# A one-pass guess matmul, and router logits, marking sum and a transpose set at other places of a hand-written order

## The chip, the cores and the metric

One NeuronCore of one Trainium2 chip. The metric is the device time of one execution in microseconds (us); lower is better. Three timed runs of the kernel before gave 402.77, 403.32 and 403.69 us, median 403.32 us.

## What is computed

Eight batches of a two-step attention, followed by a mixture of eight experts, of which each token uses one. Cut to what matters:

```python
p_packed = sm_attn(p, k, v)               # 32 packed queries per head: [8, 8, 32, 64]
out = sm_attn(q, p_packed, p_packed)      # 576 queries per head attend to the 32 packed rows
x = out as [8 * 576, 512]
logits = x @ w_gate                       # router: [4608, 8]
e_idx = argmax(logits, 1)
gate_w = softmax(logits)[e_idx]
eom = sigmoid(x @ w_output_gate)
out[t] = gate_w[t] * eom[t, e] * (relu(x[t] @ w1[e]) @ w2[e])   # e = e_idx[t]
```

## The kernel before, in words

The kernel bets that nearly all tokens of a batch choose the same expert. For each batch it **guesses** that expert early, runs the dense part for all 576 tokens with that expert's weights, and marks the tokens that chose another; marked tokens are computed again at the end.

For a batch b there are these pieces, each a Python generator that does one step at a time:

- `encode` (letters y, x): scores of the packed queries (`ps_s`), their softmax, its transposition (`ps_a1T`, `ps_a1r`), the **packed values' product** `ps_pp` (L272), its scaled copy `ppc` (VectorE, L277), the **transpose** `ps_ppT` (L285) and its copy `ppT` (ScalarE, L293), the packed rows' gate products `ps_pg` with their copies `pg` (L317, L321), and the guess: a matmul of `pg` with a matrix of ones (`ps_e`, L300) that sums over all packed rows, and six small VectorE steps (L305 to L311) that end in the expert's number.
- `route` (r, t): scores and softmax of the 576 queries (result `a2T`), its split into a high and a low part (`ah`, `al`), the **router logits** `ps_lg` (L398) and their transposition `L` (VectorE, L401), and then `gate`: a first part (L409 to L419, which ends in the exponential `g_ex` on ScalarE), a second part (L423 to L443, with the exponential `g_den` on ScalarE between `g_z` and the reciprocal), the **marking sum** `ps_cnt` (L446, a matmul of the one-hot choices with ones) and the marks (L450 to L457).
- `weights` (w): loads of the guessed expert's w1 and w2; w2 comes in four tiles, each split into `w2h` (ScalarE, L495) and `w2l` (L498, VectorE or GpSimd).
- `values_up` (g): `G`, the packed values times w1 (L513), split into `Gh` (ScalarE) and `Gl` (VectorE), both at the helper's lines L76 and L77.
- `ffn(b)`: the dense part. Two halves of the tokens (256 and 320); in each, eight groups of six matmuls `ps_h` (L85), evicted by ScalarE (`hT`, L579) and VectorE (L582), then the products `ps_o` with w2 (L613; L634 for the last 64 tokens), scaled and evicted by ScalarE (`ob`, L599) and stored.

One **beat** is one batch's `ffn`. Between its steps the letters of a table set what else is issued: `PLANS[b]` says, for step i of beat b, which pieces get one step more. Here y, Y, x work on encode of batches b+1, b, b+2; r and t on route of b+1 and b; w, W on weights of b+1 and b; g on values_up of b+1. Every engine executes its instructions strictly in the order in which this table issues them. The table is all the scheduling there is (`manual_schedule`).

PSUM has eight banks in two groups of four. Group "a" holds attention scores and transposes; group "f" holds `ps_h`, `ps_o`, `ps_lg`, `ps_cnt`, `ps_pg`, `ps_e` and half of `ps_G`. A matmul that opens a bank waits until the bank's last reader has finished. The arrangement of work at the end of beat b, in the second half's steps 28 to 34: product of tokens 256 to 383 (`ps_o` of 24 matmuls), then `ps_pp` of batch b+2 and `ps_G` of batch b+1, then the product of tokens 384 to 511 (again 24 matmuls, called **the last product** below), and then the first `ps_h` group of beat b+1.

Of the kernel before, what the change touches and what calls it, by code (L numbers as in the profile page):

```python
# [11 lines left out]
F32R = mybir.dt.float32r  # L12
# [7 lines left out]
P = 128  # L20
# [6 lines left out]


START = "kkvvqqkkYYYY1YY2YYY3YY4YYtYWttttttyYYt6G7GttGtWtvvqqkkvv"
BESIDE = "8:ry 9:yrr 10:yrrrt 11:yr 12:wrr 13:wrqq 14:rkk 15:r "  # L30
REST = "16:xr 17:x 18:r 19:xvv 20:x 22:x 24:x 25:xxw 26:ww 27:w 28:r 30:r 31:rxg 32:xg 33:gw 34:ww"
PLANS = ["1:GG 3:GG 5:G 6:WW 8:WWW 9:tt 10:tWW 11:Wyy 12:yy 13:tt 14:tt 15:yytt 16:tyy 17:ty 19:y 20:y 21:ryyr 22:yyr "
# [3 lines left out]
         "1:y 2:y 4:yWW 5:y 7:yy 8:ry 9:rry 10:rrry 11:ryw 12:rrw 13:rqq 14:rkkt 15:r " + REST] \  # L36
        + ["0:yW 1:y " + BESIDE + REST] * 3 \
        + ["0:yW 1:y " + BESIDE + REST.replace("16:xr", "20:r"), "0:W 8:l 18:l 20:lt 22:l 23:l 24:l 25:l 27:l 28:l 30:l"]


@with_exitstack
def tile_packed_attn_then_moe(ctx, tc, qT, kT, v, pT, w_go, w1, w2, out):


    nc = tc.nc
    B, _, _, NPAIR, HS = qT.shape
    NG, S = v.shape[1], 2 * HS
    NP = pT.shape[3]
    E, DM, DF = w1.shape[0], out.shape[1], BANK * w1.shape[1] // 2
# [12 lines left out]
    sb = ctx.enter_context(tc.tile_pool(name="sb", bufs=1))  # L62
# [5 lines left out]
    def bank(name, tag="a"):  # L68
        return pool.tile([P, BANK], F32, tag=tag, name=name, bufs=NA if tag == "a" else 8 - NA)

    def f(x):
        return x.bitcast(F32)
# [53 lines left out]
    ones = const.tile([P, P], F32R, name="ones")  # L126
# [44 lines left out]
    R, W, A, G, packed = {}, {}, {}, {}, {}  # L171
# [49 lines left out]
    def encode(b):  # L221
# [62 lines left out]
        ps = bank("ps_ppT")[:, :P]  # L284
# [11 lines left out]
        def guess(of):  # L296

            n = of.shape[1]
            ps = bank("ps_e", "f" if b else "a")[:, :n * E].rearrange("p (g e) -> p g e", e=E)
            nc.tensor.matmul(ps, f(ones), of, start=True, stop=True)  # L300
            yield
            top = sb.tile([P, 2, E], F32, tag="e_top", name="e_top", bufs=1)
            e = ps[:, 0]
            if n > 1:
                nc.vector.tensor_copy(top[:, 1], ps[:, 1])  # L305
                nc.vector.tensor_tensor(top[:, 1], ps[:, 0], top[:, 1], ALU.add)
                e = top[:, 1]
            nc.vector.max(top[:, 0], e)
            nc.vector.max_index(estar_i[:, b], top[:, 0], e)
            if b:  # L310
                nc.vector.tensor_copy(estar_all[:, b:b + 1], estar_i[:, b, 0:1])  # L311
            yield

        if b == 0:
            yield from guess(sums[:, 0:1])
# [3 lines left out]
        R[b] = pg = pgs[b % 3]  # L319
        for g in range(NG):  # L320
            (nc.vector.tensor_copy if b else nc.scalar.copy)(pg[:, g, :2 * E], ps_g[g])  # L321
        yield
        if b:
            yield from guess(pg[:, :, 0:E])

    def route(b):

# [496 lines left out]
    def place(plan, b):  # L824

        kinds = dict(x=(encode, 2), y=(encode, 1), Y=(encode, 0), r=(route, 1), t=(route, 0), u=(route, -1), w=(weights, 1), W=(weights, 0),
                     g=(values_up, 1), G=(values_up, 0), l=(first_leftover, 0))
        for c in plan:
            if c in kinds:
                piece(kinds[c][0], b + kinds[c][1])  # L830
            elif c == "d":
                store()
            elif c.isdigit():
                keep_warm(int(c))
            else:
                fetch(c)
# [68 lines left out]
```

## Time and profile before

| | |
|---|---|
| median of three runs | 403.32 us |
| the profiled execution, whole | 403.31 us |
| its span, first to last instruction | 401.6 us |
| TensorE (PE) busy | 393.9 us, 98% of the span |
| VectorE (DVE) busy | 280.5 us, 70% |
| ScalarE (ACT) busy | 180.7 us, 45% |
| GpSimd (POOL) busy | 40.5 us, 10% |
| share of PE in the chain that ended last | 95% |

The table is the profile's first part and the head of its fourth. Busy time of PE counts from the start of a matmul to its modelled end, so neighbours overlap; a matmul's real cost in a row of matmuls is the distance from its start to the next one's start.

### The profile page before, as it was taken

Reading aid. Unit: us, or ns where it says so; the run is one execution under the profiler, and the core shown is the slowest. Engines: PE = TensorE matmul, PEld = TensorE weight load, DVE = VectorE, ACT = ScalarE, POOL = GpSimd, SP = SyncE. Lnnn points to the kernel's source line nnn. Section 1 sums busy time; section 2 is a strip of 40 time slices with the busy share of each in tenths; the row PEclk is TensorE's granted clock in tenths of the full one; section 3 lists DMA queues with packets and bytes.
Section 4 is the critical chain, followed back from the end, with each engine's and each line's share of the span. In section 5 each row is a group of like instructions: output and inputs, shape, how many; then the busy total and the mean of one; then the engine's idle time right before and its main releaser. Section 6 shows DMA issues by size and latency. Waiting matters only on the chain.

```text
span 401.6 us, 9409 instructions
## 1 busy us (share of the span) xinstructions
PE 393.9 (98%) x3626; PEld 312.7 (78%) x3626; DVE 280.5 (70%) x793; ACT 180.7 (45%) x401; POOL 40.5 (10%) x37
## 2 busy tenths in 40 slices
PE   8999999999999999999999999999999999999995
PEld 2558886879679887787979888788977888798874
DVE  2679789687974977478765886749774786758640
ACT  1455637734555254533726236532645335532300
POOL 7000002420054000200002000020002000010010
PEclk9999999999999999999999999999999999999999
DMA  7899449927970399205990089503951068101921
GB/s 239 333 365 418 153 137 381 398 96 239 412 272 34 106 354 411 89 28 173 395 388 29 10 310 410 231 28 116 357 194 48 14 202 335 42 27 48 374 77 55
DMA packets 36686, 83.60 MB, mean 208 GB/s; under 512 B 3614, under 2 KB 16288, under 8 KB 36640
## 3 DMA queue, kind: packets, MB, share of 16 engines
q1 hardware_dynamic: 36464, 82.85, 55.8%
q8 instruction: 29, 0.48, 0.5%
q10 hardware_dynamic: 144, 0.13, 0.1%
q14 instruction: 17, 0.14, 0.1%
q0 software_dynamic: 32, 0.00, 0.0%
HBM read 67.76 MB, written 15.27 MB: 207 GB/s over the span
## 4 chain that ended last, share of the span: by engine, by line
PE 95%; DVE 2%; DMA 1%; ACT 1%; SPq 0%; issue 0%; DVEq 0%
PE ps_o L613 45%; PE ps_h L85 26%; PE ps_o L634 7%; PE ps_G L92 4%; PE ps_pp L92 3%; PE ps_s2T L92 2%; PE ps_s L92 2%; PE ps_a1T L251 2%; PE ps_lg L92 1%; DMA k<-in_kT_dram 1%; PE ps_lh L739 1%; PE ps_lo L739 1%; PE warm L119 0%; PE ps_e L300 0%; PE ps_h L563 0%; DVE hT L582 0%
## 5 line engine op out<-in xcount | busy, mean ns | idle before, releaser
L613 PE MATMUL ps_o<-w2h,hT 128*128 128x512 f32 x512 | 166.5, 396 | 0.0
L613 PEld LDWEIGHTS ps_o<-w2h,hT 128*128 128x128 f32 x512 | 96.1, 188 | 26.4 <-ACT Gh L76 4.2
L582 DVE SCALAR_TENSOR_TENSOR hT<-ps_h,hT 128x256 fp32r<-128x256 f32 x192 | 60.6, 350 | 58.0 <-ACT hT L579 57.4
L613 PE MATMUL ps_o<-w2l,hT 128*128 128x512 f32 x256 | 100.2, 391 | 0.0
L85 PE MATMUL ps_h<-ah,Gh 128*128 128x320 f32 (+1 forms) x252 | 77.3, 307 | 0.4 <-DVE hT L582 0.2
L85 PE MATMUL ps_h<-ah,Gl 128*128 128x320 f32 (+1 forms) x252 | 74.7, 296 | 0.0
L85 PE MATMUL ps_h<-al,Gh 128*128 128x320 f32 (+1 forms) x252 | 74.6, 296 | 0.0
L579 ACT ACTIVATE hT<-ps_h 128x320 fp32r<-128x320 f32 (+1 forms) x128 | 51.3, 414 | 44.0 <-PE ps_h L85 43.3
L498 POOL TENSOR_TENSOR w2l<-wst,w2h 128x1024 fp32r<-128x1024 f32 x13 | 31.3, 2411 | 299.1 <-ACT w2h L495 270.5
L613 PEld LDWEIGHTS ps_o<-w2l,hT 128*128 128x128 f32 x256 | 48.1, 188 | 9.7 <-DVE w2l L498 0.4
L85 PEld LDWEIGHTS ps_h<-ah,Gh 128*128 128x128 f32 x252 | 47.7, 189 | 4.8 <-issue 1.9
L85 PEld LDWEIGHTS ps_h<-al,Gh 128*128 128x128 f32 x252 | 47.8, 190 | 0.2
L85 PEld LDWEIGHTS ps_h<-ah,Gl 128*128 128x128 f32 x252 | 47.7, 189 | 0.0
L495 ACT CAST w2h<-wst 128x1024 fp32r<-128x1024 f32 (+1 forms) x33 | 33.6, 1047 | 4.3 <-PE ps_o L613 3.0
L599 ACT ACTIVATE ob<-ps_o,scm_all 128x512 f32<-128x512 f32 x27 | 18.5, 686 | 36.1 <-PE ps_o L613 32.9
L498 DVE TENSOR_TENSOR w2l<-wst,w2h 128x1024 fp32r<-128x1024 f32 (+1 forms) x20 | 23.3, 1167 | 7.3 <-ACT w2h L495 7.2
L366 ACT ACTIVATE s<-s 128x576 f32<-128x576 f32 (+2 forms) x18 | 11.4, 633 | 33.1 <-DVE s L363 33.1
L634 PE MATMUL ps_o<-w2h,hT 128*128 128x512 f32 x64 | 25.6, 400 | 0.0
L634 PE MATMUL ps_o<-w2l,hT 128*64 128x512 f32 x64 | 23.9, 394 | 0.0
L77 DVE TENSOR_TENSOR Gl<-ps_G,Gh 128x512 fp32r<-128x512 f32 x28 | 17.4, 681 | 8.0 <-ACT Gh L76 8.0
L386 ACT CAST ah<-a2T 128x576 fp32r<-128x576 f32 (+2 forms) x17 | 10.7, 640 | 24.8 <-DVE a2T L378 24.8
L243 ACT ACTIVATE a<-ps_s,nmx 128x288 f32<-128x288 f32 x32 | 15.8, 506 | 12.6 <-DVE nmx L238 12.5
(190 smaller groups left out, 429.2 us busy)
## 6 DMA issues: line engine op xcount, KB each, us to landing
w<-in_w_dram SPq DMA_DIRECT2D x36, 512.0 KB, 5.5
wst<-in_w_dram SPq DMA_DIRECT2D x36, 512.0 KB, 8.8
vt<-in_v_dram SPq DMA_DIRECT2D x16, 640.0 KB, 8.9
k<-in_kT_dram SPq DMA_DIRECT2D x14, 576.0 KB, 9.8
q<-in_qT_dram SPq DMA_DIRECT2D x14, 576.0 KB, 10.1
out_dram<-ob SPq DMA_DIRECT2D x31, 256.0 KB, 3.6
a_d<-a2T SPq DMA_DIRECT2D x16, 320.0 KB, 8.2
k<-in_kT_dram SPq DMA_DIRECT2D x4, 288.0 KB, 4.8
```

The source lines that it names most:

```text
L77: (lo_eng or nc.vector).tensor_tensor(lo, src, f(hi), ALU.subtract)
L85: res = nc.tensor.matmul(dst, a, m, start=j == 0, stop=j == len(seq) - 1)
L92: res = nc.tensor.matmul(dst, a, m, start=j == 0, stop=j == len(seqs[0]) - 1)
L243: nc.scalar.activation(a1[:, g, hf], s1[hf][g], AF.Exp, bias=nmx[g], scale=QK, accum_out=sm[:, g, hf:hf + 1])
L366: nc.scalar.activation(sf[g], sf[g], AF.Exp, scale=QK)
L495: nc.scalar.copy(h, x)
L498: eng("w", b, j).tensor_tensor(l, x, f(h), ALU.subtract)
L579: nc.scalar.activation(hT[:, :n], ps, AF.Relu)
L582: nc.vector.scalar_tensor_tensor(hT[:, d0:d0 + s1 - s0], ps[:, s0:s1], 0.0, f(hT[:, s0:s1]), op0=ALU.max, op1=ALU.subtract)
L599: nc.scalar.activation(ob, ob if b < 2 and t_ < 2 else ps, AF.Copy, scale=sc)
L613: nc.tensor.matmul(ps, a, m, start=fc == i == 0, stop=fc == FC - 1 and i == 2)
L634: nc.tensor.matmul(ps[:n], a, m, start=i == 0, stop=i == len(seq) - 1)
```

## The change

It moves four things and turns one matmul into another form.

1. For batches 1 to 7 the guess reads a copy `rows` of `pg` in the type float32r, and the ones in the same type. The copy is one more VectorE instruction.
2. In beats 2 to 6 the router logits of batch b+1 move from step 16 (beat 6: step 20) to step 31, behind the packed values' product; their transposition `L` and the gate's two parts move with them, to steps 32, 33 and 34.
3. The marking sum of batch b moves from the end of beat b-1 to step 10 of beat b, behind the guess; the marks to step 12.
4. The transpose `ps_ppT` and the copy `ppT` move from steps 0 and 1 of the next beat to steps 31 and 32, the transpose behind `ps_G`.

```diff
-BESIDE = "8:ry 9:yrr 10:yrrrt 11:yr 12:wrr 13:wrqq 14:rkk 15:r "
-REST = "16:xr 17:x 18:r 19:xvv 20:x 22:x 24:x 25:xxw 26:ww 27:w 28:r 30:r 31:rxg 32:xg 33:gw 34:ww"
+BESIDE = "8:ry 9:yrr 10:yrrr 11:yr 12:wrr 13:wrqq 14:rkk 15:r "
+REST = "16:x 17:x 19:xvv 20:x 22:x 24:x 25:xxw 26:ww 27:w 31:xxrgx 32:xrg 33:gwr 34:wrw"
...
-        + ["0:yW 1:y " + BESIDE + REST] * 3 \
-        + ["0:yW 1:y " + BESIDE + REST.replace("16:xr", "20:r"), "0:W 8:l 18:l 20:lt 22:l 23:l 24:l 25:l 27:l 28:l 30:l"]
+        + ["0:W " + BESIDE.replace("10:y", "10:yt").replace("12:", "12:t") + REST] * 4 \
+        + ["0:W 8:l 10:t 12:t 18:l 20:l 22:l 23:l 24:l 25:l 27:l 28:l 30:l"]
...
-            nc.tensor.matmul(ps, f(ones), of, start=True, stop=True)
+            nc.tensor.matmul(ps, ones if b else f(ones), of, start=True, stop=True)
...
-        yield
         if b:
-            yield from guess(pg[:, :, 0:E])
+            rows = sb.tile([P, NG, E], F32R, tag="e_top", name="rows", bufs=1)
+            nc.vector.tensor_copy(rows, pg[:, :, 0:E])
+        yield
+        if b:
+            yield from guess(rows)
```

Three lines are added ahead of `route`, so from there on a line number of the changed kernel is 3 higher.

TensorE around the last product, end of beat 4, before (rows of `ps_pp` that repeat are left out; `ps_cnt` is the marking sum, `ps_pp` the packed values' product, `ps_o` the last product):

```order
L446 MATMUL ps_cnt<-g_ohq,ones 128x160
L92 MATMUL ps_pp<-vt,a1T 32x64 x16
L92 MATMUL ps_pp<-vt,a1r 32x64 x4
L92 MATMUL ps_G<-w_3250,ppT 32x512 x8
L92 MATMUL ps_G<-w_3253,ppT 32x512 x8
L613 MATMUL ps_o<-w2h,hT 128x512
```

The same place in the changed kernel:

```order
L92 MATMUL ps_pp<-vt,a1T 32x64 x16
L92 MATMUL ps_pp<-vt,a1r 32x64 x4
L92 MATMUL ps_lg<-a2T,pg_94 32x160 x8
L92 MATMUL ps_G<-w_3260,ppT 32x512 x8
L92 MATMUL ps_G<-w_3263,ppT 32x512 x8
L285 MATMUL ps_ppT<-ident,ppc 128x128
L616 MATMUL ps_o<-w2h,hT 128x512
```

The marking sum is gone from here, the logits stand behind the packed values' product, and the transpose, which stood behind the last product, stands in front of it.

ScalarE over the same stretch, before (`low` and the first `ob` belong to the products ahead of `ps_pp`, the second `ob` is the eviction of the last product, `hT` the next beat's groups):

```order
L638 COPY low<-ps_o 64x512
L419 ACTIVATE g_ex<-g_d 128x40
L434 ACTIVATE g_den<-g_z 128x5
L599 ACTIVATE ob<-ps_o,scm_all 128x512
L76 CAST Gh<-ps_G 128x512 x4
L495 CAST w2h<-wst 128x1024 x2
L599 ACTIVATE ob<-ps_o,scm_all 128x512
L579 ACTIVATE hT<-ps_h 128x256
L293 COPY ppT<-ps_ppT 128x128
```

And in the changed kernel:

```order
L641 COPY low<-ps_o 64x512
L602 ACTIVATE ob<-ps_o,scm_all 128x512
L293 COPY ppT<-ps_ppT 128x128
L76 CAST Gh<-ps_G 128x512 x4
L498 CAST w2h<-wst 128x1024
L422 ACTIVATE g_ex<-g_d 128x40
L437 ACTIVATE g_den<-g_z 128x5
L498 CAST w2h<-wst 128x1024
L602 ACTIVATE ob<-ps_o,scm_all 128x512
L582 ACTIVATE hT<-ps_h 128x256 x8
```

The copy `ppT` now stands ahead of the four `Gh`, and the gate's two exponentials stand between the two `w2h`, ahead of the eviction of the last product.

VectorE over the same stretch in the changed kernel, of the gate's small steps only the first and last of each part; before, all the rows named `g_` stood ahead of `ppc`, and the `w2l` directly behind `Gl`:

```order
L277 TENSOR_TENSOR ppc<-ps_pp,rs 128x128
L404 STREAM_TRANSPOSE L<-ps_lg 128x160
L77 TENSOR_TENSOR Gl<-ps_G,Gh 128x512 x4
L412 TENSOR_REDUCE g_mx<-L 128x5
L420 TENSOR_TENSOR g_d<-L,g_mx 128x40
L501 TENSOR_TENSOR w2l<-wst,w2h 128x1024
L426 TENSOR_SCALAR g_cand<-g_d 128x40
L435 TENSOR_REDUCE g_z<-g_og 128x5
L585 SCALAR_TENSOR_TENSOR hT<-ps_h,hT 128x256 x8
```

`g_ex` reads `g_d`, and `g_den` reads `g_z`; a `w2l` of VectorE now stands between them.

## Rows read from the trace of the kernel before

**Rows 1.** The page: busy time of the engines, and TensorE's granted clock in 40 slices.

```profile
PE 393.9 (98%) x3626; PEld 312.7 (78%) x3626; DVE 280.5 (70%) x793; ACT 180.7 (45%) x401; POOL 40.5 (10%) x37
...
PEclk9999999999999999999999999999999999999999
```

**Rows 2.** Busy time by window, one beat: start:end, length, engines, granted clock, DMA.

```profile
216.50:263.00 46.50, 46.50 (x431) 38.04 (x431) 33.08 (x92) 21.86 (x48) 2.35 (x2) 1.00 0.56 213
```

**Rows 3.** Timeline of PE around a guess: start us, length us, instruction, count.

```profile
225.97 0.29 PE L300 MATMUL ps_e<-pg,ones 128*128 128x16 f32 x2
...
226.43 0.39 PE L613 MATMUL ps_o<-w2l,hT 128*128 128x512 f32 x1
```

**Rows 4.** Timeline of PE around marking sums, in beat 2 and in beat 4.

```profile
117.59 0.23 PE L446 MATMUL ps_cnt<-g_ohq,ones 128*128 128x160 f32 x1
...
117.92 0.39 PE L613 MATMUL ps_o<-w2l,hT 128*128 128x512 f32 x1
...
253.64 0.23 PE L446 MATMUL ps_cnt<-g_ohq,ones 128*128 128x160 f32 x1
253.80 0.65 PE L92 MATMUL ps_pp<-vt,a1T 128*32 128x64 f32 x32
```

**Rows 5.** Timeline of PE around router logits, in beats 0, 4 and 6.

```profile
43.39 0.84 PE L92 MATMUL ps_lg<-a2T,pg 128*32 128x160 f32 x16
44.05 0.63 PE L92 MATMUL ps_pp<-vt,a1T 128*32 128x64 f32 x32
...
235.61 0.75 PE L92 MATMUL ps_lg<-a2T,pg 128*32 128x160 f32 x16
236.29 0.42 PE L85 MATMUL ps_h<-ah,Gh 128*128 128x320 f32 x1
...
329.09 0.31 PE L85 MATMUL ps_h<-ah,Gl 128*128 128x320 f32 x1
...
330.26 0.31 PE L85 MATMUL ps_h<-al,Gh 128*128 128x320 f32 x1
```

**Rows 6.** Timeline of PE, last product of beat 4 to the end of beat 5's first groups.

```profile
256.93 0.50 PE L613 MATMUL ps_o<-w2h,hT 128*128 128x512 f32 x1
...
262.53 0.27 PE L285 MATMUL ps_ppT<-ident,ppc 128*128 128x128 f32 x1
262.55 0.36 PE L85 MATMUL ps_h<-ah,Gh 128*128 128x256 f32 x1
...
268.48 1.20 PE L92 MATMUL ps_s2T<-q,ppT 64*32 64x288 f32 x32
```

**Rows 7.** Timeline of ACT, end of beat 4, with what ended the idle time.

```profile
252.22 0.24 ACT L419 ACTIVATE g_ex<-g_d 128x40 f32<-128x40 f32 x1 [3.27 <-DVE g_d L417]
253.60 0.21 ACT L434 ACTIVATE g_den<-g_z 128x5 f32<-128x5 f32 x1 [1.14 <-DVE g_z L432]
...
256.24 2.05 ACT L76 CAST Gh<-ps_G 128x512 fp32r<-128x512 f32 x4 [1.66 <-PE ps_G L92]
...
260.00 1.06 ACT L495 CAST w2h<-wst 128x1024 fp32r<-128x1024 f32 x1 [0.33 <-PE ps_o L613]
262.79 0.69 ACT L599 ACTIVATE ob<-ps_o,scm_all 128x512 f32<-128x512 f32 x1 [1.73 <-PE ps_o L613]
263.55 0.38 ACT L579 ACTIVATE hT<-ps_h 128x256 fp32r<-128x256 f32 x1
263.83 0.26 ACT L293 COPY ppT<-ps_ppT 128x128 f32<-128x128 f32 x1
```

**Rows 8.** Timeline of DVE, end of beat 4.

```profile
250.10 1.21 DVE L498 TENSOR_TENSOR w2l<-wst,w2h 128x1024 fp32r<-128x1024 f32 x1
251.24 0.18 DVE L409 TENSOR_REDUCE g_mx<-L 128x5 f32<-128x40 f32 x1
...
252.22 0.18 DVE L423 TENSOR_SCALAR g_cand<-g_d 128x40 f32<-128x40 f32 x1
...
256.86 2.48 DVE L77 TENSOR_TENSOR Gl<-ps_G,Gh 128x512 fp32r<-128x512 f32 x4 [1.37 <-ACT Gh L76]
```

## The prediction

> **What bounds the kernel now.** I read the page first, then one beat by windows, then TensorE's timeline, then those of ScalarE and VectorE at the places that the change touches. The page has TensorE busy for 98% of the span, at the full granted clock in all 40 slices [rows 1]. In a whole beat it is busy 46.50 us out of 46.50, while VectorE is busy 33.08 us and ScalarE 21.86 us [rows 2]. So a beat is TensorE's own list of matmuls and nothing else, and only two things can change the time: what the list costs, and a wait that appears in it. Beats 2 to 5 are alike, so one place read in beat 4 counts four times.
>
> A step of the product costs 0.23 us: 24 of them fill 256.93 to 262.53, 5.60 us [rows 6]. A first-half group of six `ps_h` costs 0.74 us: eight of them fill 262.55 to 268.48, 5.93 us [rows 6].
>
> **What the list saves.** *Guess.* It is issued as two matmul records. From the start of the first to the start of the second product step behind them pass 0.46 us [rows 3], of which one step is 0.23, so the guess costs 0.23 us. How little can a one-pass guess cost? The trace has no such matmul with 16 columns. The nearest is the marking sum amid the product, also float32r and one record: 117.59 to 117.92, 0.33 us, less a step 0.10 [rows 4]. So the cost lies between 0 and 0.23, and I take 0.11. In beats 0, 1 and 2 the guess stands alone: 3 x 0.12 = 0.36 us saved. The Trainium skill says in FP8 and Floating Point Precision (TensorE Precision Notes) that true FP32 takes four passes through the array; by that three passes would go, and with 0.1 us for a pass, as an estimate, the sum below would come out near 404.6 us. The row decides: the whole guess costs 0.23 us, and more than that cannot be saved.
>
> *Marking sum.* Ahead of the packed values' product it takes 253.64 to 253.80, 0.16 us including the change to the small array tiles [rows 4]; its own part is between 0.05 and 0.10, I take 0.08. In beats 3 to 6 it moves behind the guess, where it takes the place of the guess's second record: two records of one type in a row, as before. So the pair costs the 0.23 us that the guess cost alone, and 4 x 0.08 = 0.32 us go. In beat 7 it stands alone in the product at 0.10 and saves nothing (0.03 lost).
>
> *Router logits.* In beats 2 to 5 they cost 0.68 us, 235.61 to 236.29 [rows 5]. Beat 0 has them next to `ps_pp`, where the array keeps its tile shape: 43.39 to 44.05, 0.66 us, part of it perhaps a wait for the softmax there [rows 5]. So joined they cost between 0.5 and 0.66; I take 0.58, 4 x 0.10 = 0.40 us saved. In beat 6 they cut a run of `ps_h` in two: 329.09 to 330.26 is 1.17 us, of which two `ps_h` steps are 0.3, so 0.87 [rows 5]; between `ps_o` and `ps_G`, which change the tile shape anyway, they cost the 0.68. That saves 0.2 us.
>
> *Transpose.* It keeps its cost of about 0.1 us on either side of the last product; I count nothing, with 0.1 us a beat each way for the bound. The extra copy `rows` lies on VectorE, ahead of a guess that has nine product steps (2 us) in front of it: nothing.
>
> Together 0.36 + 0.32 - 0.03 + 0.40 + 0.20 = **1.25 us saved**, between 0.5 and 2.
>
> **What the new order makes wait.** Behind the packed values' product all engines now get the last work of the beat in another order. Ahead of the eviction of the last product, ScalarE has to run `ppT`, four `Gh`, a `w2h`, `g_ex`, `g_den` and another `w2h`. `g_den` needs `g_z`, and that stands on VectorE behind four `Gl`, the gate's first part and a whole `w2l`. Before, both exponentials were done while the product ahead of `ps_pp` ran: ScalarE sat idle for 3.27 us until `g_d`, and again for 1.14 us until `g_z` [rows 7], and that cost nothing, since the eviction behind it was not due before 253.89.
>
> I put the start of the transpose at 0 and go along the chain, each step from the start to the start of the next:
> - transpose 0.27 long [rows 6], ScalarE sees it some 0.08 later: `ppT` at 0.35;
> - ScalarE starts its next instruction 0.1 before the end of one (`hT` is 0.38 long, the copy behind it starts 0.28 after it [rows 7]), so `ppT`, 0.26 long, puts `Gh` at 0.51;
> - `Gl` 0.62 after the first `Gh` (256.24 to 256.86 [rows 7, 8]): 1.13;
> - four `Gl`, 2.48 long, the next begins 0.07 before the end: 3.54;
> - gate's first part, 251.24 to 252.22 = 0.98 [rows 8]: 4.52;
> - the `w2l` of VectorE, 250.10 to 251.24 = 1.14 [rows 8]: 5.66;
> - gate's second part as far as `g_den`, 252.22 to 253.60 = 1.38 [rows 7, 8]: `g_den` at 7.04;
> - `g_den`, 0.21 long: `w2h` at 7.19, 1.06 long; the eviction `ob` at 8.15, 0.69 long [rows 7]: **done at 8.84**.
>
> TensorE meanwhile: the last product starts 0.1 after the transpose and takes 5.5 to 5.6, three groups of `ps_h` take 18/48 of 5.93 = 2.22 [rows 6]. So the fourth group could start at 7.85 to 7.92. Its bank is the one that the last product fills: of the four banks, the other three (logits, two of G) serve the first three groups. **It waits for the eviction, 0.9 to 1.0 us.** Behind it the groups follow at ScalarE's pace of 0.3 to 0.4 us each, faster than TensorE's 0.74, so nothing more is lost than some hundredths. Before, the same eviction began at 262.79, 0.1 us behind the product, and no group waited.
>
> This happens at the end of beats 2, 3, 4 and 5: 4 x 0.95 = **3.8 us lost**. Where beat 6 ends there is no packed product and no transpose; `Gh` starts about 1.2 us earlier against the last product, and the eviction is just in time: nothing.
>
> **Sum.** 403.31 (the profiled execution, which lies on the median of 403.32) - 1.25 + 3.8 = **405.9 us**.
>
> Other queues: SyncE issues the same transfers in the same order, the loads of w1 and w2 wait for the guess, which is ready slightly earlier, and GpSimd's `w2l` of the fourth tile runs some 5 us later than before but is used only after 18 steps of the next beat's first product, over 10 us on. `scm_all` of the next batch is first read by an eviction of the next beat's first product, 6 us later. The tail behind beat 7 is unchanged.
>
> **The rivals.**
> - *The chain is shorter than its parts, and no group waits.* Place: the eviction of the last product; price: the 3.8 us; it decides if the chain ends 1 us earlier than 8.84. For it: I added start-to-start distances from a stretch where the steps waited for nothing else, and each guess of mine is at 0.05 to 0.1. Against: seven of the eight steps are in the rows. Time: 403.31 - 1.25 = 402.1, faster. Chance 0.12.
> - *Half the wait*, 0.3 to 0.5 us a beat: gain and loss nearly cancel, 403.3 to 404. Chance 0.10.
> - *The wait spreads.* The later groups' evictions on ScalarE and VectorE start in a bunch, and each of the four groups left waits another 0.1 to 0.15 us: 0.4 to 0.6 us a beat more, some 408. For it: two engines must pass each bank. Against: each needs less than a group's time. Chance 0.07.
> - *The guess stays at two records.* Then 0.68 of the saving is missing and the rest stands: 406.5. It lies in my range and belongs to the forecast.
>
> **How the numbers follow.** The forecast, one wait of about a us in each of four beats, has 0.71. A measurement of this kernel tells 0.2%, 0.8 us, from no change, so 402.5 to 404.1 is "same". Slower by more: 0.71 and the spreading wait 0.07, 0.78. Faster: most of the first rival, 0.11. Same: 0.11. The range of the forecast is 1.25 saved (0.5 to 2) against 3.8 lost (4 x 0.7 to 4 x 1.1), 404.1 to 407.2. It reaches down to 403.5 for half of the second rival, and leaves out the faster case and the spreading wait, some 0.2 together.
>
> **What would show it.** In the profile after: the page has one guess record a batch, 7 instead of 14. In TensorE's list of waits a line of `ps_h` (L85) released by ScalarE's `ob` (L602), 4 times, about 0.95 us each. On ScalarE, `g_den` idles until `g_z` some 7 us after the transpose, and `ob` of the last product starts some 2.5 us after the product's end, not 0.1. Windows of beats 3 to 6 have TensorE busy less than their length for the first time. If no such line stands there, the first rival has won; if the groups behind the fourth wait too, the third.

## The result, and the profile of the changed kernel

| | before | changed |
|---|---|---|
| median | 403.32 us | 406.1 us |
| lowest to highest of five runs | 402.77 to 403.95 | 405.17 to 407.92 |
| the profiled execution | 403.31 us, span 401.6 | 405.17 us, span 403.5 |

The ratio is 1.0077, 95% interval 1.0061 to 1.0093: slower by 0.8%, and 0.2 us above the number predicted.

The page of the changed kernel: busy time of each engine, the granted clock in 40 slices, the chain that ended last, and one costly group (the last two numbers are its busy time and the mean of one, then the idle time in front and what ended it).

```profile
PE 393.1 (97%) x3619; PEld 311.3 (77%) x3619; DVE 280.9 (70%) x800; ACT 177.8 (44%) x401; POOL 40.5 (10%) x37
PEclk9999999999999999999999999999999999999998
PE 89%; DVE 5%; ACT 2%; DMA 1%; issue 1%; SPq 0%; ACTq 0%; DVEq 0%
L85 PE MATMUL ps_h<-ah,Gh 128*128 128x320 f32 (+1 forms) x252 | 77.1, 306 | 3.2 <-ACT ob L602 3.0
```

TensorE's busy time fell by 0.8 us against [rows 1], as a shorter list should, and yet the span is 1.9 us longer. VectorE and ScalarE now hold 7% of the chain, before 3%. The granted clock is full as before until TensorE's last matmul; it falls 2 us behind that, in the last slice.

TensorE's waits (total, times, longest):

```profile
PE ps_h L85 <- ACT ob L602: 3.0, 4, 0.7
PE warm L121 <- DVE blank L106: 1.1, 1, 1.1
PE ps_G L92 <- DMA w<-in_w_dram: 0.9, 1, 0.9
PE ps_s L92 <- DMA k<-in_kT_dram: 0.3, 1, 0.3
```

The first line is new. The others stand at the start, where loads land a little earlier or later in each execution.

Windows of two beats (length, then busy time of PE, PEld, DVE, ACT and POOL, granted clock, DMA):

```profile
168.59:215.87 47.28, 46.54 (x430) 37.93 (x429) 33.11 (x94) 21.26 (x47) 2.39 (x1) 1.00 0.55 210
215.87:263.15 47.28, 46.54 (x429) 37.95 (x428) 33.09 (x94) 21.27 (x47) 2.40 (x1) 1.00 0.56 210
```

A beat is 47.28 us long and TensorE works 46.54 of them; in [rows 2] it worked all of 46.50. VectorE does as much work as before and ScalarE no more.

The end of beat 4 on TensorE, from the transpose to the next beat's first half:

```profile
255.62 1.95 PE L92 MATMUL ps_G<-w,ppT 64*32 64x512 f32 x32
257.49 0.33 PE L285 MATMUL ps_ppT<-ident,ppc 128*128 128x128 f32 x1
...
262.93 0.39 PE L616 MATMUL ps_o<-w2h,hT 128*128 128x512 f32 x1
263.15 0.28 PE L85 MATMUL ps_h<-ah,Gh 128*128 128x256 f32 x1
...
265.19 0.28 PE L85 MATMUL ps_h<-ah,Gl 128*128 128x256 f32 x1
266.21 0.39 PE L85 MATMUL ps_h<-ah,Gh 128*128 128x256 f32 x1 [0.75 <-ACT ob L602]
...
270.00 1.20 PE L92 MATMUL ps_s2T<-q,ppT 64*32 64x288 f32 x32
```

Three groups of six `ps_h` run, and the fourth, at 266.21, waits for `ob`. The step behind 265.19 was due 0.12 later, at 265.31, so 0.90 us are lost in front of it. From the first `ps_h` to `ps_s2T` pass 6.85 us; in [rows 6] it was 5.93.

ScalarE and VectorE in the same stretch:

```profile
257.86 0.27 ACT L293 COPY ppT<-ps_ppT 128x128 f32<-128x128 f32 x1 [3.20 <-PE ps_ppT L285]
258.02 2.06 ACT L76 CAST Gh<-ps_G 128x512 fp32r<-128x512 f32 x4
259.93 1.09 ACT L498 CAST w2h<-wst 128x1024 fp32r<-128x1024 f32 x1
262.03 0.24 ACT L422 ACTIVATE g_ex<-g_d 128x40 f32<-128x40 f32 x1 [1.01 <-DVE g_d L420]
264.43 0.21 ACT L437 ACTIVATE g_den<-g_z 128x5 f32<-128x5 f32 x1 [2.16 <-DVE g_z L435]
264.54 1.03 ACT L498 CAST w2h<-wst 128x1024 fp32r<-128x1024 f32 x1
265.48 0.68 ACT L602 ACTIVATE ob<-ps_o,scm_all 128x512 f32<-128x512 f32 x1
```

```profile
258.65 2.48 DVE L77 TENSOR_TENSOR Gl<-ps_G,Gh 128x512 fp32r<-128x512 f32 x4 [2.54 <-ACT Gh L76]
261.05 0.18 DVE L412 TENSOR_REDUCE g_mx<-L 128x5 f32<-128x40 f32 x1
...
261.92 1.22 DVE L501 TENSOR_TENSOR w2l<-wst,w2h 128x1024 fp32r<-128x1024 f32 x1
263.05 0.18 DVE L426 TENSOR_SCALAR g_cand<-g_d 128x40 f32<-128x40 f32 x1
...
264.20 0.20 DVE L435 TENSOR_REDUCE g_z<-g_og 128x5 f32<-128x40 f32 x1
```

`ob` starts at 265.48, though the last of its matmuls starts at 262.93 and is 0.39 us long: 2.2 us late. In [rows 7] it started at 262.79, 0.1 us behind its last matmul. In between ScalarE sits idle for 2.16 us in front of `g_den`, because VectorE has not come to `g_z` (264.20).

**Where the time went.** By the ends of TensorE's records, from one beat's guess to the next, a beat took 46.55 us before and 47.28 after. The first half's 48 `ps_h` take 5.75 us where nothing waits and 6.76 here: 1.01 us a beat lost, 4.04 us in four, and some 0.27 us a beat won elsewhere in the list. From the end of batch 1's guess to TensorE's last matmul it is 2.28 us more, so the list has won 4.04 - 2.28 = 1.76 us: 1.49 up to the guess of batch 7, and 0.27 behind it.

### The profile page after: what moved, and what is told of

The parts are those of the page before. It is cut to its first block, busy times and chain, and to the rows that moved or that the text cites. A ratio compares the mean times of both kernels' runs of the same rounds, so it can differ in the third digit from the quotient of the medians.

```text
span 403.5 us, 9424 instructions
## 1 busy us (share of the span) xinstructions
PE 393.1 (97%) x3619; PEld 311.3 (77%) x3619; DVE 280.9 (70%) x800; ACT 177.8 (44%) x401; POOL 40.5 (10%) x37
## 4 chain that ended last, share of the span: by engine, by line
PE 89%; DVE 5%; ACT 2%; DMA 1%; issue 1%; SPq 0%; ACTq 0%; DVEq 0%
PE ps_o L616 40%; PE ps_h L85 24%; PE ps_o L637 7%; PE ps_G L92 4%; PE ps_pp L92 3%; PE ps_s L92 2%; PE ps_s2T L92 2%; PE ps_a1T L251 2%; DVE Gl L77 2%; PE warm L121 2%; PE ps_lg L92 1%; DVE w2l L501 1%; DMA w<-in_w_dram 1%; ACT w2h L498 1%; ACT ob L602 1%
## 5 line engine op out<-in xcount | busy, mean ns | idle before, releaser
L582 ACT ACTIVATE hT<-ps_h 128x320 fp32r<-128x320 f32 (+1 forms) x128 | 50.3, 414 | 36.1 <-PE ps_h L85 33.3
```

The source lines that it names most:

```text
L582: nc.scalar.activation(hT[:, :n], ps, AF.Relu)
```

## Experiments

In each, the kernel before ran beside on the same chip; ratios are to that. A beat's length below is the distance of the ends of two guesses on TensorE, in the profiled execution. The theory: the eviction of the last product waits in ScalarE's order behind `g_den`, and `g_den` on VectorE's order. The rivals: the new place of the logits and the gate costs as such; the one-pass guess costs; the early copy `ppT` costs as such.

### Only the guess

```diff
 (the kernel before)
-            nc.tensor.matmul(ps, f(ones), of, start=True, stop=True)
+            nc.tensor.matmul(ps, ones if b else f(ones), of, start=True, stop=True)
...
+            rows = sb.tile([P, NG, E], F32R, tag="e_top", name="rows", bufs=1)
+            nc.vector.tensor_copy(rows, pg[:, :, 0:E])
```

> The kernel before with the one-pass guess and its copy alone; the order stays as it was. My theory (TensorE's list gets shorter, nothing new waits): the trace of the change has the lone guess of the beats 0.12 us cheaper than before, and seven guesses stand alone here, so 0.8 to 0.9 us less than before, about 402.5 us. Rival (the extra copy on VectorE makes the guess late, or the float32r form costs as much): no change or slower, 403.3 us or more, with a wait of the guess matmul or of the small steps behind it.

Measured: 404.76 us (404.11 to 406.0), ratio 1.0029, 1.0016 to 1.0042. That is a miss: TensorE's beats got 0.127 us shorter each, as expected, and the kernel slower by a us. Its profiled execution (405.94 us) had a wait of 1.0 us in front of the logits. They stood for an eviction on ScalarE, and that for a late store:

```profile
73.68 0.69 ACT L602 ACTIVATE ob<-ps_o,scm_all 128x512 f32<-128x512 f32 x1 [3.07 <-DMA out_dram<-ob]
```

But one late store in one execution cannot explain a lowest run that is 1 us over the lowest of the kernel before (403.15 us). This stayed open until the last group of runs below.

### The copy late

```diff
-31:xxrgx 32:xrg 33:gwr 34:wrw
+31:xxrgx 32:rg 33:gwr 34:wrw
...
-        + ["0:W " + BESIDE...
+        + ["0:Wy " + BESIDE...
```

> The changed kernel with one thing put back: the copy ppT on ScalarE is issued at the first step of the next beat, behind the eviction of the last product; the transpose on TensorE stays behind G. My theory (the loss is the chain on ScalarE and VectorE that ends with the eviction of the last product): the four Gh no longer wait for the transpose, start about 1.25 us earlier (1.1 us after the start of G, as in the kernel before), and the chain ends 1.2 us earlier, just before the fourth group needs its bank. The four waits of ps_h for ob, 0.74 us each by the list of waits and 1.0 us each by the length of the eight groups, shrink to less than 0.2; 4 us less than the change, 401.5 to 402.3 us. Rival (the loss is on TensorE itself, in the transpose between G and the last product and its tile changes): the time stays at 405 to 406 us, since TensorE's order is the same.

Measured: 402.08 us (401.54 to 402.61), ratio 0.9962, 0.995 to 0.9975. This is inside the range of the theory. It beats both kernels, and no wait for `ob` is left. TensorE's order is that of the changed kernel, so its order alone is not the loss. TensorE and ScalarE at the end of beat 4:

```profile
253.62 1.95 PE L92 MATMUL ps_G<-w,ppT 64*32 64x512 f32 x32
```

```profile
254.80 2.06 ACT L76 CAST Gh<-ps_G 128x512 fp32r<-128x512 f32 x4 [2.13 <-PE ps_G L92]
...
262.25 0.68 ACT L602 ACTIVATE ob<-ps_o,scm_all 128x512 f32<-128x512 f32 x1
262.83 0.25 ACT L293 COPY ppT<-ps_ppT 128x128 f32<-128x128 f32 x1
```

`Gh` begins 1.18 us behind the start of `ps_G` here, and 2.40 us behind it in the changed kernel (255.62, 258.02). There it queues behind a copy of 0.27 us, but that copy needs a transpose that stands behind all 32 matmuls of `ps_G`. So the early copy costs the chain 1.2 us, not 0.27, more than the whole wait. A beat takes 46.27 us, which is 47.28 less the 1.01 of the wait.

### The gate back at its old place

```diff
-16:x 17:x 19:xvv ... 27:w 31:xxrgx 32:xrg 33:gwr 34:wrw
+16:xr 17:x 18:r 19:xvv ... 27:w 28:r 30:r 31:xxgx 32:xg 33:gw 34:ww
```

> The changed kernel with the router logits, their transposition and the two parts of the gate put back to steps 16, 18, 28 and 30; the marking sum stays behind the guess and the transpose and its copy stay behind G. My theory: with the exponentials out of ScalarE's queue ahead of the last eviction, and no VectorE step between, the eviction is on time although Gh is still held up by ppT; no wait of ps_h for ob, and the time is that of the kernel before less the guess (0.1 each) and the marking sum's place: 402 to 402.8 us. Rival (the copy ppT ahead of Gh alone makes the wait, since it delays everything behind it by 1.2 us): waits of some 0.5 us or more stay, 404 us or more.

Measured: 404.75 us (404.14 to 405.82), ratio 1.0037, 1.0022 to 1.0051. The waits for `ob` are gone, as the theory has it, and with them the rival; but the time is 2 us over the range. A beat takes 46.45 us, shorter than before. What is longer lies at the end: 0.7 us of waiting for the last load of `w`, 0.3 us in front of the logits of batch 7, and a last store that took 2.8 us instead of 1.7.

### A dose: the third `w2l` twice

```diff
-                eng("w", b, j).tensor_tensor(l, x, f(h), ALU.subtract)
+                for _ in range(2 if j == 2 and 3 <= b <= 6 else 1):
+                    eng("w", b, j).tensor_tensor(l, x, f(h), ALU.subtract)
```

> The changed kernel with the third w2l on VectorE issued twice for batches 3 to 6 (it writes the same values again). It stands between the two parts of the gate, inside the chain of my theory, and takes 1.13 us from start to start. My theory: each of the four waits grows by 1.1 us, the time by 4.5 us, to 410 to 411 us. Rival (the wait is set by something else, the w2h casts or TensorE's own order, and the gate's second part has slack): less than 1 us more, 406 to 407 us.

Measured: 415.47 us (414.69 to 416.78), ratio 1.0297, 1.0278 to 1.0315. The list of waits, `g_den` at the third of the four places, and some windows (the number behind POOL's is the granted clock):

```profile
PE ps_h L85 <- ACT ob L603: 8.0, 4, 2.0
```

```profile
270.52 0.21 ACT L437 ACTIVATE g_den<-g_z 128x5 f32<-128x5 f32 x1 [3.42 <-DVE g_z L435]
```

```profile
219.00:222.00 3.00, 1.26 (x11) 1.05 (x9) 2.37 (x14) 1.52 (x3) 0.30 (x1) 1.00 0.00 0
223.20:226.60 3.40, 3.40 (x18) 3.40 (x17) 1.63 (x5) 1.15 (x3) 0.87 (x1) 0.50 0.16 64
269.00:274.00 5.00, 3.00 (x25) 2.79 (x25) 3.77 (x18) 2.94 (x7) 2.27 (x1) 1.00 0.13 52
322.20:325.60 3.40, 3.40 (x18) 3.40 (x18) 1.27 (x3) 1.07 (x4) 0.47 (x1) 0.50 0.06 21
```

Each of the four waits grew from 0.74 to 2.00 us, by the 1.26 by which `g_den` now idles longer for `g_z` (3.42 us, in the changed kernel 2.16): VectorE's queue is what `ob` waits for, us for us. The time grew by 9.4, not by the 4.5 that were expected and more than the 5.0 of the waits, because behind two of the four waits the granted clock was 0.50, the lower of its two levels (1.2 GHz), for a stretch, and behind the other two it was not. The two beats with such a stretch took 50.03 and 50.05 us, the one between them, without, 48.55: 1.5 us each. Of the 1.4 us that are left, a longer last store, 3.0 us instead of 1.7, has most.

### The gate's second part ahead of the `w2l`

```diff
-33:gwr 34:wrw
+33:gwr 34:rww
```

> The changed kernel with two letters of the table exchanged: at step 34 the gate's second part now stands ahead of the third w2l on VectorE (table entry rww in place of wrw). Nothing else moves; the copy ppT stays early. Theory (the eviction ob of the last product waits on ScalarE behind g_den, and g_den for g_z on VectorE): g_z, and with it ob, comes earlier by the 1.2 us that the w2l took, more than the 0.7 to 1.0 us that ps_h waits for ob at each of four beat ends; these waits are gone and the time falls by 3 to 4 us, to 402.0 to 403.0. Rival (an early copy ppT costs by itself, whatever the gate does): the waits stay at 0.7 to 1.0 us and the time at 405.5 to 406.5.

Measured: 403.76 us (402.14 to 405.41), ratio 1.0016, 0.9999 to 1.0033. The copy is as early as in the changed kernel, and no `ps_h` waits for `ob` any more. ScalarE and VectorE, end of beat 4:

```profile
261.81 0.21 ACT L437 ACTIVATE g_den<-g_z 128x5 f32<-128x5 f32 x1 [1.14 <-DVE g_z L435]
...
262.86 0.68 ACT L602 ACTIVATE ob<-ps_o,scm_all 128x512 f32<-128x512 f32 x1
```

```profile
262.92 1.23 DVE L501 TENSOR_TENSOR w2l<-wst,w2h 128x1024 fp32r<-128x1024 f32 x1
```

`g_den` idles 1.14 us instead of 2.16. So the theory's link holds from this side too; but the time is 0.8 us over its range, with a last store of 3.3 us. A beat takes 46.49 us here, where the late copy has 46.27. The trace shows where the 0.2 us lie:

```profile
264.06 1.41 DVE L585 SCALAR_TENSOR_TENSOR hT<-ps_h,hT 128x256 fp32r<-128x256 f32 x4
```

```profile
264.29 0.28 PE L85 MATMUL ps_h<-ah,Gl 128*128 128x256 f32 x1
264.54 0.39 PE L85 MATMUL ps_h<-ah,Gh 128*128 128x256 f32 x1
```

The matmul at 264.54 opens the fifth group, in the bank of the first, 0.13 us later than due, and the step behind it is 0.10 longer. VectorE empties that bank from 264.06 on, only behind the `w2l` that now stands last. That the `w2l` is the cause is read from this order; no run tried it.

### The kernel before and the guess, once more; the new order with the old guess

The first is the kernel before with one comment line more, the second the text of the guess alone, the third the kernel with the late copy and the guess as it was (`f(ones)`, no `rows`).

> The kernel before, with a comment line more at its end and nothing else changed: what two copies of one program differ by when they are measured side by side. If only single transfers that land late scatter the times, its median is within 0.4 us of the kernel before. If each build has a time of its own (its place in memory, its own luck with transfers), it may be off by 1 us, and then the 404.76 and 404.75 us of the two kernels that were expected at some 402.5 say nothing of the guess.

> The kernel before with the one-pass guess alone, the same text that gave 404.76 us, to see whether that is its time and which waits of its profile come again. If the 1.1 us that ps_lg stood for ob (itself behind a late store), the 0.6 us for the last w and the 1.6 us of a longer last store were luck of transfers, the time is 402.4 to 403.4 here and the waits are elsewhere or gone. If the one-pass guess itself costs, it is 404.3 to 405.3 again with the same waits.

> The kernel with the whole new order and the copy ppT late (402.08 us), but with the guess of the kernel before: f32, read straight from pg, no copy rows. Theory by TensorE's records (a guess alone takes 0.128 us in f32 and 0.009 in one pass, a guess with the marking sum behind it some 0.04 to 0.12 more in f32): 0.3 to 0.9 us slower than that, 402.4 to 403.0. Rival (the one-pass guess or its copy costs 1 to 2 us somewhere, as the kernel with the guess alone would have it): 400.3 to 401.3.

Measured: the kernel before 402.97 us (ratio 0.9992, 0.998 to 1.0003), the guess alone 404.17 us (1.0018, 1.0006 to 1.003), the late copy with the old guess 402.39 us (0.9977, 0.9965 to 0.999). So a second build of one program is within 0.2 us, the guess alone is slower again, and yet the best order is, if anything, slower without it (ratio 0.9977 against 0.9962; the intervals overlap a little), and its beats are 0.10 us longer (46.37 against 46.27). So the loss of the guess alone is hardly the guess. TensorE's long wait of the first time was gone. What came again is in the last six us of the guess alone, by DMA queues and issues (packets, MB, share of the engines; size and us to landing):

```profile
q8 instruction: 1, 0.02, 1.4%
...
out_dram<-ob SPq DMA_DIRECT2D x1, 128.0 KB, 3.2
out_dram<-ob ACTq DMA_DIRECT2D x1, 128.0 KB, 3.1
```

In the kernel before the same two halves of the last store land in 1.7 and 1.8 us, and no packet of queue 8 is among them. Queue 8 loads code: 29 packets of 16 KB in every one of these kernels. In the kernel before the last of them starts 5.2 us before TensorE ends; in the profiles of the guess alone (both), the gate back, the doubled `w2l` and the gate first it starts 1.2 to 1.3 us behind TensorE's end, right at the last store, which then takes 2.7 to 3.5 us. These are the very kernels that were slower than their beats would have them. The Trainium skill says in Runtime: NRT & Kernel Launch (Instruction fetch mechanics) that instructions are fetched in blocks of 16 KiB, 256 instructions, and that crossing a block is mostly hidden. The traces agree with the size, 16 KB a packet; by these runs the one at the end is not hidden.

That the loads are TensorE's code is read from a count. The traces have 7,367 to 7,397 records of TensorE in these kernels, matmuls, weight loads and its sequencer's instructions together, and 29 blocks of 256 are 7,424. The place of the last load goes with that count. With 7,383 records (the kernel before, both builds), 7,384 (the copy late) and 7,397 (the late copy with the old guess) it starts 5.2 to 6.8 us before TensorE's end; with 7,373 (the guess alone, both) and 7,367 (the gate back) behind it. The changed kernel, the doubled `w2l` and the gate first all have 7,380, and in their profiles it starts 2.6 us before the end, behind it, and behind it.

### Moving the code load

```diff
+            elif i == 0:
+                for q in range(4):
+                    nc.tensor.matmul(ps[:, q * P:(q + 1) * P], idle[:, :P], idle[:, :P], start=True, stop=True)
```

Ten warming matmuls of 512 columns at the start become forty of 128, called the cut below: 60 instructions more (30 matmuls and their weight loads), the same columns. It was put into the guess alone, the gate first, the kernel before (as a control), and the changed kernel; the gate back and the doubled `w2l` were not tried with it.

> The kernel before with the one-pass guess alone (404.17 us when it ran last, with a 16 KB code load beside the last store, which took 3.2 us instead of 1.7), and each of the ten 512-column warming matmuls at the start cut into four of 128 columns: the same columns, 60 TensorE instructions more, so that every later instruction lies 60 places further on. The profiles show 29 such code loads for some 7,380 TensorE instructions. Theory (the last load fell behind TensorE's end because the program got shorter, and lengthens the last store): the load moves back to some 5 us before TensorE's end, as in the kernel before, the last store takes 1.7 to 1.8 us, and the time is 402.3 to 403.2. Rival (the one-pass guess or its copy costs by itself): 403.8 to 404.8, wherever the load falls.

> The changed kernel with the gate's second part ahead of the third w2l (403.76 us, no wait for ob left, last store 3.3 us beside a code load), with the same cut of the ten warming matmuls. Theory: the code load falls before TensorE's end, the last store takes 1.7 to 1.8 us and the time is 401.9 to 402.9, so that the early transpose costs nothing by itself. Rival (the early copy ppT keeps some 1 to 2 us of cost that no wait shows): 403.3 to 404.3 with a short last store.

> The kernel before with the same cut of the ten warming matmuls, as a control: what the cut does by itself. Its last code load already falls some 5 us before TensorE's end and stays hidden further ahead. Theory: within 0.4 us of the kernel before. If the cut itself gains or costs (at the start, by the clock or the loads), it shows here as 0.5 us or more, and is to be taken from the two others.

> The changed kernel itself with the same cut of the ten warming matmuls. In its profile (405.17 us) the last code load fell 2.6 us before TensorE's end and the last store took 1.7 us; its five runs went from 405.17 to 407.92 us. If the longer ones are runs in which that load slipped beside the last store, the 60 places further on hide it always: the median is 404.8 to 405.5 and no run is over 406.3; what is left over the kernel before is the wait for ob less the savings, some 1.9 us. If the scatter is of another source, the median stays at 405.8 to 406.4.

| | without | with the cut | ratio with it |
|---|---|---|---|
| the guess alone | 404.17 us, ratio 1.0018 | 402.69 us | 0.9995 (0.9982 to 1.0007) |
| the gate first | 403.76 us, ratio 1.0016 | 402.59 us | 0.9988 (0.9977 to 0.9998) |
| the kernel before | 403.2 us | 403.26 us | 1.0001 (0.999 to 1.0013) |
| the changed kernel | 406.1 us, ratio 1.0077 | 405.54 us | 1.0051 (1.0037 to 1.0065) |

The runs with and without the cut were made on different chips, so the ratios, each to the kernel before beside it, are what to compare. The control did not move, and of the two kernels with the load at their end the guess alone got 0.23% faster (0.9 us; the two intervals just touch) and the gate first 0.28% (1.1 us). In all four the last load now starts 8.7 to 9.5 us before TensorE's end, further ahead than the 5 us expected. The last store of the guess alone with the cut:

```profile
out_dram<-ob SPq DMA_DIRECT2D x1, 128.0 KB, 1.7
out_dram<-ob ACTq DMA_DIRECT2D x1, 128.0 KB, 1.8
```

So the guess alone is the same as the kernel before, not slower. It isn't faster either: what its shorter beats win, 0.7 us, is gone again between the last guess and TensorE's end, where the marked tokens are computed again. By the ends of TensorE's records, the second run of `ps_lh` there, a product with the leftover's `w`, takes 1.01 us when its load is in time (the changed kernel with the cut). It takes 1.25 in the kernel before, 2.00 in the guess alone with the cut, 1.68 in the late copy and 1.29 in the changed kernel. In the guess alone the load is issued as far ahead of the matmuls as in the kernel before, but it lands 7.5 us behind its issue instead of 6.7; why was not tried.

For the changed kernel the median is just over the expected range, and one run, the profiled one, is at 406.4; there `ps_G` waits 2.4 us at the start for a load of `w`. Its intervals with and without the cut overlap (1.0037 to 1.0065, 1.0061 to 1.0093). Without the cut its runs were 405.17, 405.26, 406.1, 407.79 and 407.92. That the long ones had the code load beside the store is likely, since two other kernels with the same count of records had it there; it is not shown, since those runs left no profile.

## Why the prediction was right

**The mechanism was the one predicted, step by step.** From the transpose's start, 257.49, the chain came out as follows (us):

| start of | predicted | measured |
|---|---|---|
| `ppT` | 0.35 | 0.37 |
| `Gh` | 0.51 | 0.53 |
| `Gl` | 1.13 | 1.16 |
| gate's first part | 3.54 | 3.56 |
| `w2l` | 4.52 | 4.43 |
| gate's second part | 5.66 | 5.56 |
| `g_den` | 7.04 | 6.94 |
| `ob` | 8.15 | 7.99 |
| `ob` done | 8.84 | 8.67 |
| the fourth group due | 7.85 to 7.92 | 7.82 |
| the fourth group starts | 8.84 | 8.72 |

Adding start-to-start distances from a stretch where the steps waited for other things was sound, with an error of 0.1 to 0.2 in 8.8. `ob` starts 2.2 us behind the product, where 2.5 were said. (One step of the sum, `g_den` to `w2h`, is 0.15 where its own rule of 0.1 before the end gives 0.11; 0.11 was measured. The sum's range is 404.1 to 407.2; the 403.5 named beside it is not made of its terms.) The loss was put at 0.95 us a beat, and is 0.90 in front of the group and 1.01 in the whole half: 4.04 us instead of 3.8. That this chain is the cause is shown from three sides: shorter by 1.2 us at either of two places (late copy, gate first) and the waits for `ob` are gone, longer by 1.26 and they grow by as much.

**The savings were put too low**, 1.25 us against 1.76, inside the stated 0.5 to 2. (The 1.76 is counted from the end of batch 1's guess, so the first of the three lone guesses is not in it.) Term by term, by the ends of TensorE's records:
- the guess alone: 0.12 taken, and right: it took 0.128 before and 0.009 after. The estimate of 404.6 us from the four passes of the Trainium skill's FP8 and Floating Point Precision (TensorE Precision Notes) is not borne out: [rows 3] has two records, and 0.12 us is all that left;
- the marking sum behind the guess: 0.08 taken for each of four, 0.04 measured for the pair. The guess starts at 226.76 and the product goes on at 226.94. The marking sum takes 0.15 us there and took 0.07 at its old place, so moving it lost 0.08 a beat; the pair wins only by the one-pass guess, which alone would have won 0.12. The beats say the same: 46.42 us in the guess alone, 46.45 in the gate back, though that one also has the transpose's 0.04:

```profile
226.76 0.17 PE L300 MATMUL ps_e<-rows,ones 128*128 128x16 f32 x1
226.79 0.32 PE L449 MATMUL ps_cnt<-g_ohq,ones 128*128 128x160 f32 x1
226.94 0.44 PE L616 MATMUL ps_o<-w2h,hT 128*128 128x512 f32 x1
```

- the logits: 0.10 a beat taken, 0.14 measured (0.68 alone, 0.54 next to `ps_pp`). To that come two things that I had counted at nothing: the transpose, 0.04 a beat, and 0.05 in the second half, at the opening of the fifth `ps_h` group. There the logits' transposition `L` stood ahead of an eviction on VectorE in the kernel before; the delay is there in the gate back too, which has `L` at the old place, and gone in the late copy;
- behind the last guess: 0.17 taken, 0.27 measured. The late copy's execution, with no wait for `ob`, won 1.49 up to the last guess, as the changed kernel did, but 1.36 in all, since its last load of `w` came later. So of the 1.76, a few tenths hang on that load.

**The sum came out closer than its parts, and that is luck.** Wait less savings is 4.04 - 1.76 = 2.3 us, where 2.55 were predicted, and the changed kernel with the code load out of the way is 2.1 us slower than the kernel before. The 2.8 us that the medians show have some 0.6 us more. By that much the median with the warming matmuls cut lies lower; that the code load makes this difference is not shown, since the intervals overlap. I had not foreseen that a code load can fall beside the last store: the text on the tail said that it is unchanged. That the measured 406.1 lies 0.2 from 405.9 comes of savings put too low and of these 0.6 us.

**The rivals.** The shorter chain and the half wait needed 0.5 to 1 us less than the rows gave, and the rows held. The wait did not spread: of the 1.01 us, 0.90 lie in front of the fourth group and 0.10 in the step behind its first matmul, and the groups behind it follow at 0.72 us, as before. "The guess stays at two records" fell at once: seven records where there were fourteen.

**What I did not see** is the cheap way out. The prediction starts its chain at the transpose, so the copy's late input is in the sum, and for the end of beat 6 it even says that without a transpose `Gh` starts about 1.2 us earlier and the eviction is just in time. It did not draw from this that the early copy alone makes the wait. With that one letter moved the same change is 0.38% faster than the kernel before, 402.08 us.

## What to carry to other kernels

Follow an eviction through its engine's queue before moving work in front of it: what counts is not how long the instructions ahead take, but the last input that any of them waits for. Here a copy of 0.27 us, placed behind a transpose that stands behind 32 matmuls, cost 1.2 us on a path with 0.3 us to spare. And where a kernel's time and its list of work disagree by a us, look at the last transfer and what shares the queues with it, with a control that adds instructions and no columns of work.

## What the runs showed of the hardware beyond that

- A 16 KB code load, TensorE's by the count above, that fell beside the last 256 KB of stores made them land in 2.7 to 3.5 us instead of 1.7 to 1.8. With 60 TensorE instructions more at the start it fell 8.7 us or more before TensorE's end; the two kernels got 0.9 and 1.1 us faster by their ratios, and the control did not change (0.06 us).
- Waits of TensorE of 0.74 us left the granted clock at full; of four waits of 2.00 us in one execution two were followed by a stretch at half clock, 1.5 us lost each time, and two were not.
